# One two-input product for the softmax scaling, and two small statistics kept as extra columns, in a windowed attention that feeds a soft mixture of experts

## The chip, the core and the metric

The kernel runs on one core of one Trainium2 chip. The core has TensorE for matmuls (PE; its weight loads are listed as PEld), VectorE (DVE), ScalarE (ACT), GpSimd (POOL) and SyncE (SP), which here only issues transfers. The metric is the device time of one execution in microseconds (us). The kernel before took 297.65 us, the median of three runs of 295.35, 297.65 and 297.83 us.

## The reference

The program is an attention with a causal window of 128 positions and a linear distance bias per head, followed by a soft mixture of experts over all 4608 tokens (8 batches of 576).

```
scores = scale * q @ k.T ;  rel = i - j
scores = where((rel >= 0) & (rel < 128), scores - slope[h] * |rel|, -1e9)
attn   = exp(scores - max) ;  attn /= sum + 1e-9        # softmax along a row
x      = attn @ v                                        # 4608 tokens x 512
logits = x @ phi                                         # 32 slots
d = exp(logits - max over tokens) ;  d /= sum over tokens + 1e-9
slot_input = d.T @ x ;  slot_out = relu(slot_input @ w1) @ w2   # 8 experts, 4 slots each
c = exp(logits - max over slots)  ;  c /= sum over slots + 1e-9
out = c @ slot_out
```

## The kernel before, in words

A batch of 576 tokens is cut into four tiles of 128 tokens and a tail of 64. A tile's eight heads are done in two groups of four, the tail's in one, so that a batch has nine groups and the whole front part 72 (`groups`). One iteration of the loop over `groups` does these steps, each for another group, so that several groups are in flight:

- `softmax_front(new, old)` on DVE: `merge` (L267, L269, L271) masks the new scores in PSUM, `rowmax` (L289) takes each row's maximum, `inverse` (L301) turns the old group's row sums into reciprocals, `bias` (L292) scales the maximum for the exponential, and `normalise` (L306) multiplies the old group's four 128x128 blocks P, one instruction for each, by their reciprocals. `total` (L297) adds EPS to the sums, on GpSimd.
- `flip` (L351): four transposes of P on TensorE for the group three back. `split`: ScalarE copies the result to SBUF (L358), and GpSimd makes two masked copies of it with an affine select each (L360 for the part of the window in the previous tile, L362 for the part in its own; L365 and L367 for the tail).
- `values` (L387): P times v on TensorE for the group four back, which reads both masked copies; ScalarE stores the tile of x (`x_store`, L403).
- `scores` (L247 and L254, L235 and L240 in a batch's first tile) of the next group on TensorE.
- `expo` (L341): four exponentials on ScalarE, each with its row sums (the ACTIVATION_READ_ACCUMULATOR rows).

Beside that, once a batch, with steps spread over the iterations by `after_values`: x is flipped (`x_flip`, L408, kept by ScalarE at L417) and multiplied with phi (`logits`, L426; copied at L444 and L446). The statistics over tokens are kept as running values: `token_max` takes the maximum of the batch's logits (L451), joins it with the running one (L453) and negates it (L455). The running maximum stands in two columns that take turns, `mn` and `mo`. `token_exp` takes the exponentials on ScalarE (L475, L479), and `slot_add` (L522) adds the batch's share to the slots' inputs. The statistics over slots are in `ln`, 32 numbers for each token: `slots_max`, `slots_exp`, and `slots_norm`, which has four small DVE steps (L543 the sums, L544 adding EPS, L545 the reciprocals, L546 the product). These four go into a list `fillers`, of which `softmax_front` takes one at each of four places: behind `merge`, behind `rowmax`, behind `inverse` and behind `bias`.

The order on each engine is the order in which the code issues (`manual_schedule`): an engine works its list strictly from the front, and an instruction that waits holds up all behind it on that engine. The weights for the experts stream in all the while. After the front part come the experts (`hidden`, L931; `expert_out`, L967) and the mixing of their outputs (`combine`, L991, with copies at L993 and stores of the result).

Of the kernel before, what the change touches and what calls it, by code (L numbers as in the profile page):

```python
# [10 lines left out]
F32 = mybir.dt.float32  # L11
# [12 lines left out]
NS = E * SPE  # L24
P = 128
# [43 lines left out]
def tile_attn_softmoe(  # L69
# [24 lines left out]
    unit_r = cpool.tile([P, P], F32R, name="unit_r")  # L94
    ident = unit_r.bitcast(F32)
    fine = cpool.tile([P, 14], F32, name="fine")
    low, m_run, s_run = fine[:, 0:1], fine[:, 1:3], fine[:, 3:4]
    comb = cpool.tile([P, NS], F32, name="comb")
    phi = cpool.tile([P, NPAIR, NS], F32, name="phi")
    lg = cpool.tile([P, HW], F32, name="lg")  # L100
    ln = cpool.tile([P, NTT, NS], F32, name="ln")
    acc = cpool.tile([P, DM], F32, name="acc")
    kq = cpool.tile([P, 3 * UW], F32, name="kq")
    ramp = cpool.tile([P, 2, 2, WIN], BF16, name="ramp")
# [91 lines left out]
    with tc.manual_schedule(engines=ORDERED):  # L196
        warm = area[:, 2].bitcast(BF16)[:, 0:512]
        nc.vector.memset(warm, 0.0)
        nc.vector.memset(low, LOW)
        nc.vector.memset(ramp, 0.0)  # L200
        nc.vector.memset(ones, 1.0)
        nc.vector.memset(fine[:, 10:11], -1.0)
        nc.gpsimd.memset(cst[:, 0:P], 1.0)
        nc.gpsimd.affine_select(cst[:, 0:P], cst[:, 0:P], [[1, P]], ALU.is_gt, 0.0, base=0, channel_multiplier=-1)
        load_k(0, 0)
        load_q(0, nc.scalar)
        for par in range(2):
            nc.sync.dma_start(ramp[64 * par:64 * par + 1], slopes[par:par + 1])
        load_q(1, nc.scalar)
        load_q(2, nc.scalar)  # L210
        load_k(0, 1)
        tiny = work.tile([P, 1], F32, tag="nm", name="tiny")
        nc.scalar.activation(tiny, low, AF.Exp)
        for i in range(WARM):
            nc.tensor.matmul(free[i % 4], lhsT=warm[:, 0:P], rhs=warm, start=True, stop=True)
        nc.gpsimd.memset(lg, LOW)
        nc.gpsimd.memset(area[:, 3, 0:P], 1.0)
        nc.gpsimd.affine_select(
            unit_r, area[:, 3, 0:P], [[1, P]], ALU.is_equal, 0.0, base=0, channel_multiplier=-1)
        load_v()  # L220
        nc.scalar.dma_start(cst[:, P:], cstd)
        nc.scalar.dma_start(phi, phid)
        for t in range(2, NT):
            load_k(0, t)
# [75 lines left out]
    def inverse(key, us):  # L300
        nc.vector.reciprocal(st[key]["rs"][:, us], st[key]["rs"][:, us])  # L301

    def normalise(key, us, mul=nc.vector.tensor_scalar_mul):
        p4 = st[key]["p4"]
        for u in range(4)[us]:
            mul(p4[:, u], p4[:, u], st[key]["rs"][:, u:u + 1])  # L306

    fillers = []

# [4 lines left out]
    def softmax_front(new, old):  # L314
# [4 lines left out]
            total(old, ALL, nc.gpsimd)  # L319
        if first:  # L320
            inverse(old, ALL)
            normalise(old, LO, nc.scalar.mul)
        rowmax(new, ALL)
        filler()
        if not first and not eager:
# [93 lines left out]
    def lanes(b):  # L419
        return 4 if b < last else 2  # L420
# [11 lines left out]
    def with_tail(b):  # L432
        return b % 2 and b < last
# [12 lines left out]
            nc.scalar.copy(lg[fin, P:2 * P], lp[fin, P:2 * P])  # L446

    def token_max(b):
        odd, r = b % 2, NS * lanes(b)
        mo, mn = m_run[:, 1 - odd:2 - odd], m_run[:, odd:odd + 1]  # L450
        nc.vector.tensor_reduce(mn[0:r], lg[0:r, 0:P * (2 if with_tail(b) else 1)], axis=AX.X, op=ALU.max)  # L451
        if b:
            nc.vector.tensor_tensor(mn[0:r], mn[0:r], mo[0:r], op=ALU.max)  # L453
        nm = work.tile([P, 1], F32, tag="nm", name="nm")
        nc.vector.tensor_scalar_mul(nm[0:r], mn[0:r], -1.0)  # L455
        if r < P:
            nc.gpsimd.tensor_copy(mn[r:P], mo[r:P])
        st["n", b] = nm

    def slot_flip(b):  # L460
# [7 lines left out]
        st["c", b], st["lm"] = lq, dp  # L468

    def token_exp(b):  # L470
        odd, r = b % 2, NS * lanes(b)
        m = P * (2 if with_tail(b) else 1)
        nm = st.pop(("n", b))
        sb = work.tile([P, 1], F32, tag="sb", name="sb")
        nc.scalar.activation(lg[0:r, 0:m], lg[0:r, 0:m], AF.Exp, bias=nm[0:r], scale=1.0, accum_out=sb[0:r])  # L475
        al = None
        if b:
            al = work.tile([P, 1], F32, tag="al", name="al")
            nc.scalar.activation(al[0:r], m_run[0:r, 1 - odd:2 - odd], AF.Exp, bias=nm[0:r], scale=1.0)  # L479
        st["s", b] = (al, sb)  # L480

    def token_sum(b):
# [35 lines left out]
    def slot_add(b):  # L518
# [4 lines left out]
        else:  # L523
            nc.vector.tensor_copy(acc, ap)

    def slots(b):
        return ln[:, 9 * (b // 2) + 4 * (b % 2):9 * (b // 2) + 4 + 5 * (b % 2)]

    def slots_max(b):
        m = 4 + b % 2  # L530
# [8 lines left out]
    def slots_norm(b):  # L539
        m = 4 + b % 2  # L540
        cs = work.tile([P, 5], F32, tag="cs", name="cs")
        return [
            lambda: nc.vector.tensor_reduce(cs[:, 0:m], slots(b), axis=AX.X, op=ALU.add),  # L543
            lambda: nc.vector.tensor_scalar_add(cs[:, 0:m], cs[:, 0:m], EPS),  # L544
            lambda: nc.vector.reciprocal(cs[:, 0:m], cs[:, 0:m]),  # L545
            lambda: nc.vector.tensor_tensor(slots(b), slots(b), bc(cs[:, 0:m], 2, NS), op=ALU.mult),  # L546
        ]

    def later(fn, b):
# [12 lines left out]

    def lane_rows(to):
        lane_bank.extend([to[0:1, 0:2 * P], to[:, 2 * P:2 * P + 3]])
        nc.tensor.transpose(to[0:1, 0:P], m_run[:, last % 2:last % 2 + 1], ident)
        nc.tensor.transpose(to[0:1, P:2 * P], s_run, ident)

    def lane_values(i):
# [553 lines left out]
```

## Time and profile before

| | us |
|---|---|
| median of three runs | 297.65 |
| lowest and highest run | 295.35 and 297.83 |
| span of the profiled execution, first to last instruction | 294.4 |
| TensorE busy | 275.9 (94% of the span) |
| VectorE busy | 240.3 (82%) |
| ScalarE busy | 208.2 (71%) |
| GpSimd busy | 93.0 (32%) |

The profiled execution's own time outside its span is not shown; its span is 0.95 us under the fastest run and 3.25 us under the median. The loop over groups runs from about 6 to 222 us, the end of the front part to about 238.6 us, and the experts from there to the end. "Busy" is the time in which at least one instruction of an engine runs. Matmuls are pipelined and their ends are modelled, so TensorE's share can also hide short waits. A row of a timeline gives start, length, engine, line, operation, output and inputs, how many instructions are merged into it, and in brackets how long the engine was idle before and what ended that.

### The profile page before, as it was taken

The numbers are of one execution on the slowest core, as the hardware profiler recorded it, in microseconds if no ns is written. First come the engines' busy times: TensorE is split into PE (matmuls) and PEld (weight loads), VectorE is DVE, ScalarE is ACT, GpSimd is POOL, SyncE is SP. The second block draws the span as 40 slices with busy tenths as digits, with TensorE's granted clock in tenths as the row PEclk, the third lists the DMA queues.
The fourth block names the chain that finished last, engine by engine and source line by source line (L and its number), as shares of the span: only waits on it lengthen the run. The fifth ranks groups of instructions, "written<-read, shape, count | busy, mean of one in ns | idle before, by whom it ended". The sixth has DMA issues, their size and how long they took to land. (4 is left out here: it accounts for less than half of the span.)

```text
span 294.4 us, 13061 instructions
## 1 busy us (share of the span) xinstructions
PE 275.9 (94%) x5131; PEld 195.7 (66%) x5131; DVE 240.3 (82%) x745; ACT 208.2 (71%) x814; POOL 93.0 (32%) x207
## 2 busy tenths in 40 slices
PE   8598999999999999999999999999999999999980
PEld 4366777777677777776776777667766743587650
DVE  3889999999989999998999999979996454655450
ACT  2778898987988988987898978978886421044450
POOL 2033525542444354244415442445452011000000
PEclk9689999999999999999999999999999999999997
DMA  6635368878676887868588967776456599998997
GB/s 192 217 112 144 110 194 251 277 218 288 203 265 209 268 284 235 260 213 273 180 281 262 292 217 248 248 222 222 141 164 234 160 314 355 411 400 327 345 365 264
DMA packets 36754, 72.59 MB, mean 247 GB/s; under 512 B 4402, under 2 KB 15316, under 8 KB 36692
## 3 DMA queue, kind: packets, MB, share of 16 engines
q1 hardware_dynamic: 35972, 71.24, 72.8%
q8 instruction: 41, 0.67, 0.9%
q10 hardware_dynamic: 720, 0.51, 0.6%
q14 instruction: 21, 0.17, 0.2%
HBM read 62.29 MB, written 9.44 MB: 244 GB/s over the span
## 5 line engine op out<-in xcount | busy, mean ns | idle before, releaser
L341 ACT ACTIVATE area<-s,nb 128x128 f32<-128x128 f32 x288 | 102.3, 375 | 19.8 <-DVE nb L292 17.5
L306 DVE TENSOR_SCALAR area<-area,rs 128x128 f32<-128x128 f32 x286 | 79.5, 339 | 0.7 <-DVE nb L292 0.3
L387 PE MATMUL xp<-area 128*64 128x128 f32 (+1 forms) x1104 | 75.4, 272 | 1.1 <-POOL rs L297 0.4
L387 PEld LDWEIGHTS xp<-area 128*64 128x64 f32 x1104 | 56.5, 137 | 15.9 <-issue 9.3
L341 ACT ACTIVATION_READ_ACCUMULATOR area<-s,nb 128x1 f32 x288 | 61.3, 213 | 0.0
L289 DVE TENSOR_REDUCE s<-s 128x4 f32<-128x512 f32 x71 | 49.5, 698 | 2.2
L358 ACT COPY area<-pt 128x512 f32<-128x512 f32 (+1 forms) x72 | 42.3, 590 | 11.6 <-PE pt L351 11.3
L351 PE MATMUL pt<-unit_r,area 128*128 128x128 f32 x282 | 45.9, 285 | 2.7 <-ACT area L306 2.2
L297 POOL TENSOR_SCALAR rs<-sm 128x4 f32<-128x4 f32 x70 | 13.8, 197 | 99.0 <-ACT area L341 98.2
L351 PEld LDWEIGHTS pt<-unit_r,area 128*128 128x128 f32 x282 | 32.0, 143 | 17.2 <-PE s L254 5.0
L254 PE MATMUL s<-kq 64*32 64x160 f32 x1792 | 42.4, 303 | 0.1
L360 POOL TENSOR_SCALAR_AFFINE_SELECT area<-area 128x512 f32<-128x512 f32 x48 | 31.4, 655 | 26.7 <-ACT area L358 25.6
L269 DVE COPY_PREDICATED s<-cst,s 128x512 f32<-128x512 int32 x48 | 32.9, 686 | 1.3 <-PE s L254 1.3
L362 POOL TENSOR_SCALAR_AFFINE_SELECT area<-area 128x512 f32<-128x512 f32 x48 | 31.5, 657 | 3.3
L254 PEld LDWEIGHTS s<-kq 64*32 64x32 f32 x1792 | 29.9, 108 | 1.0 <-issue 0.4
L408 PE MATMUL xq<-unit_r,area 128*128 128x128 f32 x136 | 22.1, 285 | 0.8 <-ACT area L417 0.7
L403 ACT COPY area<-xp 128x512 f32<-128x512 f32 (+1 forms) x37 | 20.7, 559 | 2.9 <-PE xp L387 2.3
L247 PE MATMUL s<-ramp,ones 64*32 64x320 bf16 x448 | 18.9, 313 | 2.7 <-ACT area L341 2.2
L417 ACT COPY area<-xq 128x512 f32<-128x512 f32 x34 | 20.7, 608 | 0.2 <-PE xq L408 0.2
L408 PEld LDWEIGHTS xq<-unit_r,area 128*128 128x128 f32 x136 | 14.5, 141 | 7.4 <-issue 4.1
L993 ACT COPY ob<-po 128x512 f32<-128x512 f32 x19 | 10.4, 591 | 11.4 <-PE po L991 10.7
L993 DVE COPY ob<-po 128x512 f32<-128x512 f32 x17 | 11.2, 687 | 6.6 <-PE po L991 5.8
(169 smaller groups left out, 328.4 us busy)
## 6 DMA issues: line engine op xcount, KB each, us to landing
w<-w SPq DMA_DIRECT2D x53, 512.0 KB, 5.2
out<-ob SPq DMA_DIRECT2D x36, 256.0 KB, 3.9
kq<-q_t SPq DMA_DIRECT2D x69, 128.0 KB, 3.2
kq<-k_t SPq DMA_DIRECT2D x32, 256.0 KB, 3.8
area<-v_n SPq DMA_DIRECT2D x31, 256.0 KB, 4.2
area<-w SPq DMA_DIRECT2D x8, 512.0 KB, 4.8
area<-v_n SPq DMA_DIRECT2D x12, 128.0 KB, 3.1
kq<-w SPq DMA_DIRECT2D x3, 512.0 KB, 6.3
```

Source lines behind the costliest of these rows:

```text
L254: nc.tensor.matmul(s4[32 * c:32 * c + 32, 2 * par + jj, 32 * r:32 * r + WIN], lhsT=qt[rows, 2 * h + jj if t == 4 else jj, 32 * r:32 * r + 32],
L269: nc.vector.copy_predicated(s4[:, :, P:2 * P], bc(mask_u, 1, 4), s4[:, :, 0:P])
L289: nc.vector.tensor_reduce(st[key]["mx"][:, us], merged(key, us), axis=AX.X, op=ALU.max, negate=True)
L306: mul(p4[:, u], p4[:, u], st[key]["rs"][:, u:u + 1])
L341: nc.scalar.activation(s["p4"][:, u], merged(key, u), AF.Exp, bias=s["nb"][:, u:u + 1], scale=SCALE, accum_out=s["sm"][:, u:u + 1],)
L351: nc.tensor.transpose(s["pt"][:, u], s["p4"][:, u], ident)
L358: nc.scalar.copy(pa[:, us], s["pt"][:, us])
L360: nc.gpsimd.affine_select(pp[:, us], pa[:, us], [[0, m], [-1, P]], ALU.is_gt, 0.0, base=0, channel_multiplier=1)
L362: nc.gpsimd.affine_select(pa[:, us], pa[:, us], [[0, m], [1, P]], ALU.is_ge, 0.0, base=0, channel_multiplier=-1)
L387: nc.tensor.matmul(xp[D * par:D * par + D, j, 0:w], lhsT=v_slot[b, t - 1 + ph][0:rows, D * h:D * h + D], rhs=src[:, 2 * par + i] if t < 4 ...
L408: nc.tensor.transpose(xq[:, P * j:P * j + P], x_of(b, t)[:, j], ident)
L993: copy_by[by](ob, po)
```

## The change

Three things change. The product of P with its reciprocals becomes one `tensor_tensor` over all four blocks, whose second input is the column of reciprocals repeated along the row. Only the first two blocks of the very first group are still scaled one at a time on ScalarE. Then the running token maximum is stored in the column just ahead of the logits, in the same tile, so that one `tensor_reduce` over the logits and that column gives the joined maximum, already negated; GpSimd writes it back with its sign turned once `token_exp` has read the old one. And each token's 32 slot values get a 33rd column that holds EPS from the start, so that the sum includes it; the product of slot values and reciprocals goes to GpSimd for all batches but the last.

```diff
-    low, m_run, s_run = fine[:, 0:1], fine[:, 1:3], fine[:, 3:4]
+    low, s_run = fine[:, 0:1], fine[:, 3:4]
...
-    lg = cpool.tile([P, HW], F32, name="lg")
-    ln = cpool.tile([P, NTT, NS], F32, name="ln")
+    lgm = cpool.tile([P, 4 + HW], F32, name="lg")
+    m_run, lg = lgm[:, 3:4], lgm[:, 4:]
+    lne = cpool.tile([P, NTT, NS + 1], F32, name="ln")
+    ln = lne[:, :, 0:NS]
...
-        nc.gpsimd.memset(lg, LOW)
+        nc.gpsimd.memset(lgm, LOW)
+        nc.gpsimd.memset(lne[:, :, NS:NS + 1], EPS)
...
-    def normalise(key, us, mul=nc.vector.tensor_scalar_mul):
+    def normalise(key, us):
+        p4, rs = st[key]["p4"][:, us], st[key]["rs"][:, us]
+        nc.vector.tensor_tensor(p4, p4, bc(rs, 2, P), op=ALU.mult)
+
+    def normalise_first(key, us):
         p4 = st[key]["p4"]
         for u in range(4)[us]:
-            mul(p4[:, u], p4[:, u], st[key]["rs"][:, u:u + 1])
+            nc.scalar.mul(p4[:, u], p4[:, u], st[key]["rs"][:, u:u + 1])
...
     def token_max(b):
-        odd, r = b % 2, NS * lanes(b)
-        mo, mn = m_run[:, 1 - odd:2 - odd], m_run[:, odd:odd + 1]
-        nc.vector.tensor_reduce(mn[0:r], lg[0:r, 0:P * (2 if with_tail(b) else 1)], axis=AX.X, op=ALU.max)
-        if b:
-            nc.vector.tensor_tensor(mn[0:r], mn[0:r], mo[0:r], op=ALU.max)
+        r = NS * lanes(b)
         nm = work.tile([P, 1], F32, tag="nm", name="nm")
-        nc.vector.tensor_scalar_mul(nm[0:r], mn[0:r], -1.0)
-        if r < P:
-            nc.gpsimd.tensor_copy(mn[r:P], mo[r:P])
+        nc.vector.tensor_reduce(
+            nm[0:r], lgm[0:r, 3:4 + P * (2 if with_tail(b) else 1)], axis=AX.X, op=ALU.max, negate=True)
         st["n", b] = nm
...
-            nc.scalar.activation(al[0:r], m_run[0:r, 1 - odd:2 - odd], AF.Exp, bias=nm[0:r], scale=1.0)
+            nc.scalar.activation(al[0:r], m_run[0:r], AF.Exp, bias=nm[0:r], scale=1.0)
+        nc.gpsimd.tensor_scalar(m_run[0:r], nm[0:r], -1.0, 1.0, op0=ALU.mult, op1=ALU.mult)
...
     def slots_norm(b):
         m = 4 + b % 2
         cs = work.tile([P, 5], F32, tag="cs", name="cs")
+        mul = (nc.gpsimd if b < last else nc.vector).tensor_tensor
         return [
-            lambda: nc.vector.tensor_reduce(cs[:, 0:m], slots(b), axis=AX.X, op=ALU.add),
-            lambda: nc.vector.tensor_scalar_add(cs[:, 0:m], cs[:, 0:m], EPS),
+            lambda: nc.vector.tensor_reduce(cs[:, 0:m], lne[:, rows(b)], axis=AX.X, op=ALU.add),
             lambda: nc.vector.reciprocal(cs[:, 0:m], cs[:, 0:m]),
-            lambda: nc.vector.tensor_tensor(slots(b), slots(b), bc(cs[:, 0:m], 2, NS), op=ALU.mult),
+            lambda: mul(slots(b), slots(b), bc(cs[:, 0:m], 2, NS), op=ALU.mult),
         ]
```

The first place to look at is VectorE's list in the iteration of an even batch that takes the fillers. `area` holds P, `rs` its reciprocals, `s` the scores, `nb` the bias, `ln` and `cs` the slot values and their sums. Before:

```order
L267 COPY_PREDICATED s_1_83<-cst,fine 128x4x128
L543 TENSOR_REDUCE cs<-ln 128x4
L289 TENSOR_REDUCE s_1_83<-s_1_83 128x4
L544 TENSOR_SCALAR cs<-cs 128x4
L301 RECIPROCAL rs<-rs 128x4
L545 RECIPROCAL cs<-cs 128x4
L292 TENSOR_SCALAR nb<-s_1_83 128x4
L546 TENSOR_TENSOR ln<-ln,cs 128x128
L306 TENSOR_SCALAR area<-area,rs 128x128 x4
```

The same iteration on VectorE now:

```order
L270 COPY_PREDICATED s_1_83<-cst,fine 128x4x128
L550 TENSOR_REDUCE cs<-ln 128x4
L292 TENSOR_REDUCE s_1_83<-s_1_83 128x4
L551 RECIPROCAL cs<-cs 128x4
L304 RECIPROCAL rs<-rs 128x4
L295 TENSOR_SCALAR nb<-s_1_83 128x4
L308 TENSOR_TENSOR area<-area,rs 128x512
```

Between the masking and the bias the step that added EPS is gone, and the slots' reciprocals stand one place earlier; behind the bias the product of the slots is gone, and one product stands where four scalings stood.

The second place is GpSimd's list in the same iteration: `rs` are the sums of the group whose exponentials were taken last, and the pair of affine selects behind it makes the masked copies in `area` that `values` reads in the next iteration. Before:

```order
L297 TENSOR_SCALAR rs<-sm 128x4
L360 AFFINE_SELECT area<-area 128x512
L362 AFFINE_SELECT area<-area 128x512
L297 TENSOR_SCALAR rs<-sm 128x4
L365 AFFINE_SELECT area<-area 128x512
```

The same place on GpSimd now:

```order
L300 TENSOR_SCALAR rs<-sm 128x4
L552 TENSOR_TENSOR ln<-ln,cs 128x4x32
L367 AFFINE_SELECT area<-area 128x512
L369 AFFINE_SELECT area<-area 128x512
L300 TENSOR_SCALAR rs<-sm 128x4
L372 AFFINE_SELECT area<-area 128x512
```

The product of the slots now stands ahead of the pair of selects, and it waits for VectorE's reciprocals `cs`. In the same way the write of the running maximum (`lg<-nm 128x1`, L482 of the changed kernel) stands once a batch behind a pair of selects. TensorE's list is the same in both kernels.

More of the change, by code (lines that the diff above doesn't have):

```diff
@@ L321, in softmax_front @@
             inverse(old, ALL)
-            normalise(old, LO, nc.scalar.mul)
+            normalise_first(old, LO)
         rowmax(new, ALL)
@@ L470, in token_exp @@
     def token_exp(b):
-        odd, r = b % 2, NS * lanes(b)
+        r = NS * lanes(b)
         m = P * (2 if with_tail(b) else 1)
@@ L524, in slot_add, with rows @@
             nc.vector.tensor_copy(acc, ap)
+    def rows(b):
+        return slice(9 * (b // 2) + 4 * (b % 2), 9 * (b // 2) + 4 + 5 * (b % 2))
     def slots(b):
-        return ln[:, 9 * (b // 2) + 4 * (b % 2):9 * (b // 2) + 4 + 5 * (b % 2)]
+        return ln[:, rows(b)]
     def slots_max(b):
@@ L564, in lane_rows @@
         lane_bank.extend([to[0:1, 0:2 * P], to[:, 2 * P:2 * P + 3]])
-        nc.tensor.transpose(to[0:1, 0:P], m_run[:, last % 2:last % 2 + 1], ident)
+        nc.tensor.transpose(to[0:1, 0:P], m_run, ident)
         nc.tensor.transpose(to[0:1, P:2 * P], s_run, ident)
```

## Prediction

> **What bounds the kernel now.** I read the busy time by stage first: start, loop over groups, end of the front part, experts. The columns are TensorE, its weight loads, VectorE, ScalarE and GpSimd, each with busy us and instructions, then granted clock, DMA share and GB/s.
>
> ```profile
> core 0: us, PE busy (x) PEld busy (x) DVE busy (x) ACT busy (x) POOL busy (x), PEclk, DMA share, GB/s
> 0.00:30.00 30.00, 23.93 (x414) 16.20 (x415) 22.61 (x72) 19.75 (x81) 7.61 (x24) 0.89 0.57 169
> 30.00:210.00 180.00, 177.95 (x3668) 130.99 (x3666) 171.67 (x542) 155.02 (x638) 74.87 (x161) 1.00 0.74 236
> 210.00:238.60 28.60, 26.75 (x321) 19.11 (x320) 19.03 (x65) 18.52 (x67) 9.09 (x19) 1.00 0.60 195
> 238.60:294.40 55.80, 47.23 (x734) 29.41 (x733) 26.98 (x69) 14.89 (x30) 1.48 (x4) 0.96 0.93 349
> ```
>
> In the loop VectorE is busy 171.67 of 180 us, which by itself makes it look like the engine to relieve. But TensorE is busy 177.95, at full clock: only 2.05 us are left there. Since that share can hide waits, I looked next at TensorE's own timeline over one iteration.
>
> ```profile
> 110.44 0.60 PE L351 MATMUL pt<-unit_r,area 128*128 128x128 f32 x4
> ...
> 112.66 0.66 PE L351 MATMUL pt<-unit_r,area 128*128 128x128 f32 x4
> 113.24 1.09 PE L387 MATMUL xp<-area 128*64 128x128 f32 x16
> 114.33 0.33 PE L247 MATMUL s<-ramp,ones 64*32 64x320 bf16 x8
> 114.47 0.74 PE L254 MATMUL s<-kq 64*32 64x160 f32 x32
> 115.14 0.66 PE L408 MATMUL xq<-unit_r,area 128*128 128x128 f32 x4
> 115.63 0.60 PE L351 MATMUL pt<-unit_r,area 128*128 128x128 f32 x4
> 116.16 1.09 PE L387 MATMUL xp<-area 128*64 128x128 f32 x16
> ...
> 99.98 1.29 PE L254 MATMUL s<-kq 64*32 64x160 f32 x32
> ...
> 26.26 0.33 PE L247 MATMUL s<-ramp,ones 64*32 64x320 bf16 x8 [1.28 <-ACT area L341]
> ...
> 220.33 0.66 PE L408 MATMUL xq<-unit_r,area 128*128 128x128 f32 x4 [0.65 <-ACT area L417]
> ...
> 223.19 0.27 PE L465 MATMUL dp<-unit_r,lg 64*128 64x64 f32 x1 [0.62 <-ACT lg L444]
> ```
>
> From 112.66 to 116.16 each row begins before the one ahead has ended, or at once: TensorE works without a pause through a whole iteration. Hidden waits exist, but they are few: the 32 score matmuls take 0.74 us as a rule and 1.29 us at 99.98, so 0.55 us are hidden there. So two engines are nearly full, and the one that is not touched is the fuller. What the change can win is only TensorE's waits: 2.05 us in the loop and, as an estimate from rows like that at 99.98, as much again hidden; 28.60 − 26.75 = 1.85 us at the end of the front part; and the 1.28 us at 26.26. The sum, about 7 us, is the ceiling, however much VectorE gets back.
>
> **The change part by part.** First VectorE's durations. The groups' columns are count, busy us and mean ns; the timeline shows one scaling of P with GpSimd quiet, one with it at work, and the iteration with the fillers.
>
> ```profile
> L306 DVE TENSOR_SCALAR area<-area,rs 128x128 f32<-128x128 f32 x286 | 79.5, 339 | 0.7 <-DVE nb L292 0.3
> L691 DVE TENSOR_TENSOR cstk<-ln,cstk 128x256 fp32r<-128x256 f32 x9 | 3.8, 426 | 0.3
> L453 DVE TENSOR_TENSOR fine<-fine 128x1 f32<-128x1 f32 x6 | 2.1, 347 | 0.2
> L546 DVE TENSOR_TENSOR ln<-ln,cs 128x160 f32<-128x160 f32 x4 | 2.1, 527 | 0.0
> L546 DVE TENSOR_TENSOR ln<-ln,cs 128x128 f32<-128x128 f32 x4 | 2.0, 504 | 0.0
> L544 DVE TENSOR_SCALAR cs<-cs 128x5 f32<-128x5 f32 x4 | 1.5, 379 | 0.0
> L534 DVE TENSOR_TENSOR ln<-dp,cm 128x128 f32<-128x128 f32 x4 | 1.2, 292 | 0.1
> L544 DVE TENSOR_SCALAR cs<-cs 128x4 f32<-128x4 f32 x4 | 1.2, 301 | 0.0
> L455 DVE TENSOR_SCALAR nm<-fine 128x1 f32<-128x1 f32 x7 | 1.1, 154 | 0.2
> ```
>
> ```profile
> 112.61 1.25 DVE L306 TENSOR_SCALAR area<-area,rs 128x128 f32<-128x128 f32 x4
> 112.68 0.71 POOL L362 TENSOR_SCALAR_AFFINE_SELECT area<-area 128x512 f32<-128x512 f32 x1
> 113.78 0.69 DVE L267 COPY_PREDICATED s<-cst,fine 128x512 f32<-128x512 int32 x1
> 114.83 0.63 POOL L360 TENSOR_SCALAR_AFFINE_SELECT area<-area 128x512 f32<-128x512 f32 x1 [0.27 <-ACT area L358]
> 115.17 0.32 DVE L544 TENSOR_SCALAR cs<-cs 128x4 f32<-128x4 f32 x1
> 115.53 0.63 POOL L362 TENSOR_SCALAR_AFFINE_SELECT area<-area 128x512 f32<-128x512 f32 x1
> 115.73 0.57 DVE L546 TENSOR_TENSOR ln<-ln,cs 128x128 f32<-128x128 f32 x1
> 115.84 0.37 ACT L341 ACTIVATE area<-s,nb 128x128 f32<-128x128 f32 x1 [1.08 <-DVE nb L292]
> 116.23 0.86 DVE L306 TENSOR_SCALAR area<-area,rs 128x128 f32<-128x128 f32 x4
> ```
>
> The product of P. Four scalings take 0.86 us undisturbed (116.23) and 1.25 us beside a select of GpSimd (112.61); the mean is 79.5 / (286 / 4) = 1.11 us a group. No row shows the new product, 128x512. A product of 128 elements takes 292 ns and one of 256 takes 426 ns, so 134 ns for each 128 more, and 426 + 2 × 134 = 694 ns. It too has two SBUF inputs, and such a one waits for GpSimd: at 115.73 a product of 128 takes 0.57 us, 0.28 more than the 292 ns, and ends just behind the select that ends at 116.16. The bounds are 0.70 and 0.98 us; I take 0.90, nearer to the disturbed row because the iterations are alike. That is 0.21 us less in each of 70 groups, 14.7 us.
>
> The small steps. L453 and L455 vanish (2.1 + 1.1 us), as does L544 (1.5 + 1.2), and of L546 seven of eight products leave VectorE, all but one of 160 elements undisturbed (2.1 + 2.0 − 0.3). That is 9.7 us; the reductions grow by one column in 128 or by one in 32, which I cost at nothing. So VectorE goes from 240.3 to about 216 us, and in the loop from 171.7 to some 150 us, under ScalarE's 155.0. In time, this buys only what TensorE waited for on its account. Of the loop's 4 us I take half, 2.0: the waits come mostly through exponentials that start late, as at 115.84, where ScalarE stood 1.08 us for a bias that the fillers had delayed, and these start earlier now. Of the 1.28 us at 26.26 I take 0.5, since the exponentials there also queue behind a copy that waits for TensorE itself, and of the 0.65 and 0.62 us at the end of the front part 0.5, since the VectorE step ahead of them waits for matmuls. Gain: 3.0 us. Its bounds are 0 and 7.
>
> What GpSimd gets. Here are the nearest rows for its new work, and one select beside a VectorE instruction with two SBUF inputs.
>
> ```profile
> L204 POOL TENSOR_SCALAR_AFFINE_SELECT cst<-cst 128x128 f32<-128x128 f32 x1 | 0.3, 292 | 0.1
> L1023 POOL TENSOR_SCALAR ostk<-cst 128x64 fp32r<-128x64 f32 x2 | 0.7, 380 | 0.0
> L362 POOL TENSOR_SCALAR_AFFINE_SELECT area<-area 128x512 f32<-128x512 f32 x48 | 31.5, 657 | 3.3
> ```
>
> ```profile
> 215.90 0.69 DVE L267 COPY_PREDICATED s<-cst,fine 128x512 f32<-128x512 int32 x1
> 216.13 0.94 POOL L360 TENSOR_SCALAR_AFFINE_SELECT area<-area 128x512 f32<-128x512 f32 x1 [0.31 <-ACT area L358]
> ```
>
> The write of the running maximum, one column, stands behind a pair of selects and ahead of sums that wait for exponentials anyway: nothing, and 0.3 us a batch if that cover were gone. The product of the slots stands ahead of a pair of selects. It waits for VectorE's reciprocals, the selects queue behind it, and `values` on TensorE waits for them. Its own length lies between 0.29 us (one input, 128 elements) and 0.66 us; I take 0.45. In the iteration above, the reciprocals can come no earlier than 115.17 − 113.78 + 0.18 = 1.57 us behind the masking's start. That start is 113.78 because VectorE was late; scores were there by 112.7, so with the time won I put it at 113.1. Then the reciprocals are there at 114.7, the product ends at 115.2, the pair (0.63 + 0.07 + 0.63) at 116.5, and `values` wants its second half 0.1 us behind 116.16 (two of its 16 matmuls in 1.09 us): some 0.25 us late. If the product of P takes its turn between the two selects, they end 0.3 us later still (0.94 for 0.63 at 216.13). I take 0.5 us, bounds 0 and 0.9, in the three even batches of the loop; in odd ones a flip of x lies between and covers it. New waits: 1.5 us, bounds 0 and 5.
>
> The sum against the profiled execution: 294.4 − 3.0 + 1.5 = 292.9 us of span. What lies around the span isn't in the profile, and the fastest run is 0.95 us and the median 3.25 us above it, so I apply the difference of −1.5 us to the median: 297.65 − 1.5 = 296.1 us.
>
> **The rivals.** *All of it counts* (293.2 us). The selects start earlier by as much as they are delayed, and TensorE's visible waits of 2.05 + 1.85 us and 0.6 at the start go. For it speaks that ScalarE's copies ahead of the selects were themselves late behind late exponentials. Against it speaks that GpSimd's pair ends at 116.16, exactly where `values` begins: there is no slack today. 297.65 − 4.5 = 293.2.
>
> *GpSimd becomes the wait* (303 us, slower). Four short scalings let a select in between any two: at 112.68 it takes 0.71 us, hardly more than 0.63. One long product does not, and a select costs 0.3 us more, as at 216.13. If that reaches TensorE in half of the 48 pairs, it costs 7.2 us; with 1.5 for the slots and 3.0 won, 297.65 + 5.7 = 303. It decides where a pair ends more than 0.1 us behind the start of `values`. Against it: the pair has about an iteration of cover in most groups, and only the short iterations (one lasts from 110.44 to 112.66, 2.22 us) have none. The Trainium skill, page "SBUF — State Buffer", section "SBUF: two separate sides", says that VectorE with two SBUF inputs and GpSimd share a port pair as an exclusive lock, held for the whole instruction. By that rule the product of P shuts GpSimd out for all of its length, and the trace agrees at 216.13 in one direction and at 115.73 in the other.
>
> *The product isn't shorter* (299 us). If it loses its turn to both selects, it takes 0.70 + 2 × 0.28 = 1.26 us against 1.11; in some 62 groups of the loop that is 9 us more on VectorE against 8 saved by the small steps. VectorE stays full, the new waits stay, and nothing is won: 297.65 + 1.5. Against it: four scalings could lose four turns, one product hardly two. The Trainium skill, page "VectorE: DVE Perf Modes", section "The perf-mode tier table", gives fp32 scalings from SBUF twice the rate of a two-input product, which speaks against the change. With that page's formula of 58 cycles and one per element (half for the scaling), an estimate is 0.51 us for four scalings and 0.59 us for the product; the trace has 0.86 us for the four, so the fixed part of each weighs more here than the page says.
>
> **How the numbers follow.** Forecast 0.55 (its own range 294.3 to 298), all of it counts 0.27, GpSimd becomes the wait 0.12, the product isn't shorter 0.06. A difference under 1%, 3 us, can hardly be told from none here, as the three runs of before lie 2.5 us apart. Faster by over 1% (under 294.7) is the first rival and 0.05 of the forecast: 0.32. Slower by over 1% (over 300.6) is 0.10 of the second rival and 0.02 of the third: 0.12. The rest, 0.56, is within 1%. The range reaches from 292.6, a little under the first rival, to 300.0, which leaves out most of the second.
>
> **What would show it.** Right: the product of P at 0.7 to 1.0 us; VectorE at about 216 us busy and its share in the loop under ScalarE's; TensorE's steps as long as before and its busy time in the loop at 98% or more, so that the span moves little; in even batches a wait of `values` for the second select behind the slots' product. Wrong: `values` waiting for selects in many iterations; the product over 1.1 us; a slots' product on GpSimd of over 1 us; or TensorE's steps themselves getting shorter, which would mean that what I read as its own rate was a wait in disguise, and that the ceiling of 7 us was none.

## The result and the profile after

The changed kernel takes 298.34 us, the median of 20 runs (296.65 to 301.40). The kernel before takes 296.83 us in 20 runs on the same chip (294.61 to 302.44). The ratio is 1.0061, with a 95% interval of 1.0040 to 1.0082. So the kernel became slower by 0.6%, about 1.8 us. That is within the 1% called "the same" above, but the forecast was 1.5 us faster.

The profiled execution has a span of 296.3 us, against 294.4 before. The busy time by stage, with the columns and stages of the first table in the prediction, now reads:

```profile
0.00:30.00 30.00, 22.91 (x426) 15.47 (x427) 21.51 (x53) 21.05 (x87) 9.95 (x26) 0.94 0.56 172
30.00:210.00 180.00, 174.99 (x3580) 127.30 (x3578) 153.78 (x337) 153.64 (x628) 85.90 (x170) 1.00 0.74 235
210.00:240.60 30.60, 29.31 (x401) 20.90 (x396) 18.18 (x46) 19.26 (x72) 10.44 (x23) 1.00 0.56 178
240.60:296.30 55.70, 47.58 (x737) 29.72 (x736) 26.67 (x67) 14.91 (x30) 1.96 (x5) 0.96 0.93 355
```

In the loop VectorE went from 171.67 to 153.78 us of 180, so the relief that was meant is there. TensorE went from 177.95 to 174.99, which is 97% of the stretch: it waits 3 us more, and gets through 3580 of its instructions in this stretch, where it was 3668. GpSimd went from 74.87 to 85.90. The groups of VectorE and GpSimd that moved, each with count, busy us and mean ns, then idle time before and what ended it:

```profile
L308 DVE TENSOR_TENSOR area<-area,rs 128x512 f32<-128x512 f32 x70 | 59.1, 845 | 2.0
L270 DVE COPY_PREDICATED s<-cst,fine 128x512 f32<-128x512 int32 x15 | 12.5, 835 | 0.0
L489 DVE SCALAR_TENSOR_TENSOR fine<-fine,al,sb 128x1 f32<-128x1 f32 x6 | 3.5, 583 | 0.0
```

```profile
L369 POOL TENSOR_SCALAR_AFFINE_SELECT area<-area 128x512 f32<-128x512 f32 x48 | 36.2, 754 | 3.3
L367 POOL TENSOR_SCALAR_AFFINE_SELECT area<-area 128x512 f32<-128x512 f32 x48 | 35.4, 738 | 29.2 <-ACT area L365 26.2 <-PE xp L394 2.8
L374 POOL TENSOR_SCALAR_AFFINE_SELECT area<-area 64x512 f32<-64x512 f32 x7 | 6.9, 991 | 0.5
L552 POOL TENSOR_TENSOR ln<-ln,cs 128x128 f32<-128x128 f32 x4 | 1.6, 400 | 6.1 <-DVE cs L551 4.2 <-DVE rs L304 1.8
L552 POOL TENSOR_TENSOR ln<-ln,cs 128x160 f32<-128x160 f32 x3 | 1.4, 456 | 1.9 <-DVE rs L304 1.9
L482 POOL TENSOR_SCALAR lg<-nm 128x1 f32<-128x1 f32 x7 | 1.3, 184 | 0.0
```

The product of P takes 0.845 us, where four scalings took 1.11. Against that, the selects of GpSimd grew from about 655 ns to 738 and 754, and the tail's from 663 to 991. The slots' product takes 0.40 us for a batch of four tiles and 0.46 us for one of five, and GpSimd stood idle ahead of it for VectorE's reciprocals.

To see where the time went, I matched TensorE's 5131 weight loads of the two traces, which come in the same order, and took for each the difference of its start. Negative is earlier than before. The table has the larger steps, not all:

| place (us in the trace after) | shift ahead, us | shift behind, us | step |
|---|---|---|---|
| first 34 us | 0 | −1.33 | −1.33 |
| iteration with the fillers, batch at 60 | −0.86 | −0.05 | +0.81 |
| the same, at 90 | −0.61 | +0.24 | +0.85 |
| the same, at 116 | −0.33 | +0.44 | +0.77 |
| the same, at 145 | −0.11 | +0.74 | +0.85 |
| `values` at 158 | +0.46 | +1.60 | +1.14 |
| fillers, at 173 | +1.33 | +2.11 | +0.78 |
| fillers, at 202 | +1.56 | +2.27 | +0.71 |
| `values` at 209 | +2.27 | +2.71 | +0.44 |
| end of the front part | +2.71 | +2.21 | −0.50 |

The six iterations that take the fillers lose 0.7 to 0.9 us each, 4.8 us together, odd batches as much as even ones. Between them 0.3 to 0.6 us are won back, and 0.47 us of the lead at 34 us is lost again by 60. Of what is won back between 90 and 116, 0.49 us is not the change's: it is the row at 99.98 in the prediction, 32 score matmuls in 1.29 us. They take 0.73 us here and in all nine experiments below, whether P has one product, two, four scalings or none, so that wait belongs to the one execution of the kernel before that was profiled.

```profile
99.92 0.73 PE L257 MATMUL s<-kq 64*32 64x160 f32 x32
```

This is the first of the six iterations; a timeline's columns are those of the prediction:

```profile
58.46 0.20 POOL L300 TENSOR_SCALAR rs<-sm 128x4 f32<-128x4 f32 x1 [0.73 <-ACT area L348]
58.99 0.16 DVE L551 RECIPROCAL cs<-cs 128x4 f32<-128x4 f32 x1
59.24 0.40 POOL L552 TENSOR_TENSOR ln<-ln,cs 128x128 f32<-128x128 f32 x1 [0.59 <-DVE rs L304]
59.32 0.86 DVE L308 TENSOR_TENSOR area<-area,rs 128x512 f32<-128x512 f32 x1
59.59 1.09 POOL L367 TENSOR_SCALAR_AFFINE_SELECT area<-area 128x512 f32<-128x512 f32 x1
...
60.74 0.44 PE L394 MATMUL xp<-area 128*64 128x128 f32 x4 [0.25 <-POOL area L367]
60.75 0.64 POOL L369 TENSOR_SCALAR_AFFINE_SELECT area<-area 128x512 f32<-128x512 f32 x1
...
61.45 0.88 PE L394 MATMUL xp<-area 128*64 128x128 f32 x12 [0.27 <-POOL area L369]
```

GpSimd has done the sums by 58.66 and then waits 0.59 us for VectorE, with the two selects queued behind. The slots' product runs from 59.24. When it ends, VectorE's product of P, which started at 59.32, is still running, and the first select takes 1.09 us instead of 0.64: it ends 0.50 us behind the end of the product of P at 60.18. `values` (L394) waits for the first select and then again for the second; the two waits are 0.52 us of the step, and its 16 matmuls, cut in two, take 0.44 + 0.88 = 1.32 us instead of 1.09. An odd batch looks the same:

```profile
88.25 0.46 POOL L552 TENSOR_TENSOR ln<-ln,cs 128x160 f32<-128x160 f32 x1 [0.63 <-DVE rs L304]
88.66 1.09 POOL L367 TENSOR_SCALAR_AFFINE_SELECT area<-area 128x512 f32<-128x512 f32 x1
...
90.51 0.88 PE L394 MATMUL xp<-area 128*64 128x128 f32 x12 [0.27 <-POOL area L369]
```

The two steps in `values` itself, at 158 and 209, are of another kind:

```profile
158.34 0.44 PE L394 MATMUL xp<-area 128*64 128x128 f32 x4 [0.87 <-issue]
...
209.47 0.88 PE L394 MATMUL xp<-area 128*64 128x128 f32 x12 [0.96 <-DMA area<-v_n]
```

At 209 the wait is for a block of v. Five of the experiments below wait there too, 0.92 to 1.50 us, the longest in the kernel that changes only the token column; three others wait 0.16 to 0.39 us. The kernel without scaling and the kernel before show no such wait in their one trace each. At 158 the row names no releaser, and what it waits for stays open. A row without a releaser at that place is 0.55 us long in one experiment and 0.27 in another, and none stands there in the others. Neither wait follows the change, and I did not test them.

### The profile page after: what moved, and what is told of

Its sections match the earlier page's. It is cut to its first block, busy times and chain, and to the rows that moved or that the text cites. A ratio compares the mean times of both kernels' runs of the same rounds, so it can differ in the third digit from the quotient of the medians.

```text
span 296.3 us, 12828 instructions
## 1 busy us (share of the span) xinstructions
PE 274.8 (93%) x5131; PEld 193.4 (65%) x5131; DVE 220.1 (74%) x502; ACT 208.9 (70%) x814; POOL 108.3 (37%) x222
## 5 line engine op out<-in xcount | busy, mean ns | idle before, releaser
L394 PE MATMUL xp<-area 128*64 128x128 f32 (+1 forms) x1104 | 77.1, 273 | 5.0 <-POOL area L369 1.6
L394 PEld LDWEIGHTS xp<-area 128*64 128x64 f32 x1104 | 56.1, 136 | 21.9 <-issue 10.2
L348 ACT ACTIVATION_READ_ACCUMULATOR area<-s,nb 128x1 f32 x288 | 63.3, 220 | 0.0
L308 DVE TENSOR_TENSOR area<-area,rs 128x512 f32<-128x512 f32 (+1 forms) x73 | 60.4, 828 | 2.1
L358 PE MATMUL pt<-unit_r,area 128*128 128x128 f32 x282 | 45.2, 282 | 3.6 <-ACT area L313 2.6
L367 POOL TENSOR_SCALAR_AFFINE_SELECT area<-area 128x512 f32<-128x512 f32 x48 | 35.4, 738 | 29.2 <-ACT area L365 26.2
L257 PE MATMUL s<-kq 64*32 64x160 f32 x1792 | 41.1, 298 | 0.0
L369 POOL TENSOR_SCALAR_AFFINE_SELECT area<-area 128x512 f32<-128x512 f32 x48 | 36.2, 754 | 3.3
L257 PEld LDWEIGHTS s<-kq 64*32 64x32 f32 x1792 | 29.2, 106 | 0.6 <-issue 0.2
L270 DVE COPY_PREDICATED s<-cst,fine 128x512 f32<-128x512 int32 (+1 forms) x17 | 13.4, 788 | 3.9 <-issue 3.9
```

The lines of the kernel that those rows point to most:

```text
L257: nc.tensor.matmul(s4[32 * c:32 * c + 32, 2 * par + jj, 32 * r:32 * r + WIN], lhsT=qt[rows, 2 * h + jj if t == 4 else jj, 32 * r:32 * r + 32],
L308: nc.vector.tensor_tensor(p4, p4, bc(rs, 2, P), op=ALU.mult)
L348: nc.scalar.activation(s["p4"][:, u], merged(key, u), AF.Exp, bias=s["nb"][:, u:u + 1], scale=SCALE, accum_out=s["sm"][:, u:u + 1],)
L358: nc.tensor.transpose(s["pt"][:, u], s["p4"][:, u], ident)
L367: nc.gpsimd.affine_select(pp[:, us], pa[:, us], [[0, m], [-1, P]], ALU.is_gt, 0.0, base=0, channel_multiplier=1)
L369: nc.gpsimd.affine_select(pa[:, us], pa[:, us], [[0, m], [1, P]], ALU.is_ge, 0.0, base=0, channel_multiplier=-1)
```

## The experiments

My theory was that the slots' product, by its place in GpSimd's list, is the loss: it waits for VectorE ahead of the urgent selects. The rival was the product of P: long and with two SBUF inputs, it holds up GpSimd's selects everywhere. Ratios are to the kernel before in runs on the same chip, with 95% intervals. The first four kernels ran on one chip (before: 296.06 us, 30 runs), the next four on another (before: 295.93 us, 35 runs), the last on a third.

### The slots' product stays on VectorE

```diff
-        mul = (nc.gpsimd if b < last else nc.vector).tensor_tensor
+        mul = nc.vector.tensor_tensor
```

> The changed kernel with the slots' product on VectorE for all batches (in its place among the fillers); the rest as changed. Queue theory: in the changed kernel the product of the slots stands ahead of the pair of selects on GpSimd and waits for VectorE's reciprocals, and this costs TensorE 0.8 us in each of six iterations. Without it the waits of values behind late selects in these iterations vanish, 6 x 0.8 = 4.8 us less, and VectorE gets back 0.3 to 0.6 us an iteration that it can spare: 293.5 to 294.5 us, 1% under the kernel before. Port theory: what costs is the long product of P, which holds the port against the selects everywhere; then nothing much changes, 298 us.

Measured: 295.35 us, ratio 0.9970 (0.9945 to 0.9994). All of the change except this one move is 0.3% faster than before; so the loss comes with the move. The time is nearer to the queue theory, but under neither expectation: the waits behind the slots' product are gone, while each of the six tails of the loop now loses some 0.3 us, as in the next kernel.

### The product of P alone

The kernel before, with the new `normalise` and nothing else of the change.

```diff
-    def normalise(key, us, mul=nc.vector.tensor_scalar_mul):
+    def normalise(key, us):
+        p4, rs = st[key]["p4"][:, us], st[key]["rs"][:, us]
+        nc.vector.tensor_tensor(p4, p4, bc(rs, 2, P), op=ALU.mult)
...
-            mul(p4[:, u], p4[:, u], st[key]["rs"][:, u:u + 1])
+            nc.scalar.mul(p4[:, u], p4[:, u], st[key]["rs"][:, u:u + 1])
```

> The kernel before with the one product for P alone; token maximum and slots as before. Queue theory: only gains are left, the faster start and the shorter waits for late exponentials: 1.5 to 2.5 us under the kernel before, 294.5 to 295.5. Port theory: the loss is all here, 1 to 2 us over the kernel before.

Measured: 296.50 us, ratio 1.0002 (0.9977 to 1.0027). That is between the two expectations, and neither came true. VectorE is busy 225.3 us instead of 240.3, and none of it arrives. The groups and one tail of a batch show a part of what takes it. First the kernel with the product alone, groups and then the timeline:

```profile
L305 DVE TENSOR_TENSOR area<-area,rs 128x512 f32<-128x512 f32 x70 | 55.3, 791 | 2.2 <-DVE nb L292 1.0
L366 POOL TENSOR_SCALAR_AFFINE_SELECT area<-area 128x512 f32<-128x512 f32 x48 | 35.7, 743 | 3.3
L371 POOL TENSOR_SCALAR_AFFINE_SELECT area<-area 64x512 f32<-64x512 f32 x7 | 7.2, 1026 | 0.5
```

```profile
62.92 0.69 DVE L305 TENSOR_TENSOR area<-area,rs 128x512 f32<-128x512 f32 x1
63.12 1.02 POOL L371 TENSOR_SCALAR_AFFINE_SELECT area<-area 64x512 f32<-64x512 f32 x1
...
64.19 1.47 PE L391 MATMUL xp<-area 64*64 64x64 f32 x28 [0.42 <-POOL area L371]
```

And the same place in the kernel before:

```profile
63.79 1.34 DVE L306 TENSOR_SCALAR area<-area,rs 128x128 f32<-128x128 f32 x4
63.80 0.66 POOL L367 TENSOR_SCALAR_AFFINE_SELECT area<-area 64x512 f32<-64x512 f32 x1
```

Who yields has changed. Beside four short scalings the select went at full speed (0.66 us) and VectorE paid (1.34 instead of 0.86). Here the one product, which started first, goes at full speed (0.69) and the select pays (1.02). In most iterations the select has time to spare; in the tail it has none, and `values`, which ran on there without such a wait, waits 0.42 us. By the shifts of TensorE's weight loads, this kernel loses 0.36 to 0.39 us in each of the six tails of the loop. It is also 0.9 us ahead of before at 34 us; that this lead comes from the product is not shown (see below, on the gain). In the changed kernel the tail's select is as slow, but it starts at 62.48 instead of 63.12, since the exponentials come earlier, and `values` hardly waits. The groups of the tail's matmuls, first with the product alone, then in the changed kernel:

```profile
L391 PE MATMUL xp<-area 64*64 64x64 f32 x112 | 6.3, 230 | 2.7 <-POOL area L371 2.7
L394 PE MATMUL xp<-area 64*64 64x64 f32 x112 | 6.3, 230 | 0.2 <-POOL area L374 0.2
```

### The slots' product on GpSimd alone

The kernel before, with this one move.

```diff
-            lambda: nc.vector.tensor_tensor(slots(b), slots(b), bc(cs[:, 0:m], 2, NS), op=ALU.mult),
+            lambda: (nc.gpsimd if b < last else nc.vector).tensor_tensor(slots(b), slots(b), bc(cs[:, 0:m], 2, NS), op=ALU.mult),
```

> The kernel before with the slots' product on GpSimd alone (EPS still added by its own VectorE step, four scalings of P). Queue theory: the loss is here, 3 to 5 us over the kernel before, 300 to 302, since the reciprocals come even later than in the changed kernel. Port theory: within 0.5 us of the kernel before.

Measured: 299.57 us, ratio 1.0107 (1.0070 to 1.0145), 3.2 us slower. Here P still has its four scalings, so the rival's mechanism is not in this kernel at all, and the loss is.

```profile
60.45 0.43 POOL L546 TENSOR_TENSOR ln<-ln,cs 128x128 f32<-128x128 f32 x1 [1.11 <-DVE nb L292]
60.84 0.63 POOL L360 TENSOR_SCALAR_AFFINE_SELECT area<-area 128x512 f32<-128x512 f32 x1
61.53 0.44 PE L387 MATMUL xp<-area 128*64 128x128 f32 x4 [0.57 <-POOL area L360]
...
62.30 0.88 PE L387 MATMUL xp<-area 128*64 128x128 f32 x12 [0.33 <-POOL area L362]
```

GpSimd waits 1.11 us here, since VectorE still has the step that adds EPS, and `values` waits 0.57 us and 0.33 us, though the selects keep nearly their length (654 and 663 ns in the mean). So the wait for VectorE is enough for a loss of this size, without a select that is drawn out.

### The slots' product behind the selects

The changed kernel, in which the product of slots and reciprocals stays on GpSimd but is issued behind the pair of selects of the same iteration (for the first six batches).

```diff
-            lambda: mul(slots(b), slots(b), bc(cs[:, 0:m], 2, NS), op=ALU.mult),
...
+    def slots_scale(b):
+        m = 4 + b % 2
+        nc.gpsimd.tensor_tensor(slots(b), slots(b), bc(st["cs", b][:, 0:m], 2, NS), op=ALU.mult)
...
+            if b < last - 1:
+                do("act", i + 7, slots_scale, b)
```

> The changed kernel with the slots' product still on GpSimd, but issued behind the pair of selects of the same iteration (for the loop's six batches). Queue theory: its inputs are there by then and nothing urgent is queued behind it, so the 4.8 us go: 293 to 294.5 us. Port theory: the same instructions hold the port for the same time, 298 us.

Measured: 294.55 us, ratio 0.9934 (0.9905 to 0.9963). The same work on the same engine, one place further back: 1.27% less than the changed kernel, 3.8 us, with the two intervals put together 2.7 to 4.8 us.

```profile
59.41 0.63 POOL L367 TENSOR_SCALAR_AFFINE_SELECT area<-area 128x512 f32<-128x512 f32 x1 [0.27 <-ACT area L365]
59.83 0.76 DVE L308 TENSOR_TENSOR area<-area,rs 128x512 f32<-128x512 f32 x1
60.12 0.97 POOL L369 TENSOR_SCALAR_AFFINE_SELECT area<-area 128x512 f32<-128x512 f32 x1
60.39 0.60 PE L358 MATMUL pt<-unit_r,area 128*128 128x128 f32 x4
...
60.92 1.09 PE L394 MATMUL xp<-area 128*64 128x128 f32 x16
61.06 0.39 POOL L560 TENSOR_TENSOR ln<-ln,cs 128x128 f32<-128x128 f32 x1
```

The first select starts at 59.41, at once when ScalarE's copy is there, and runs ahead of the product of P. The second pays 0.34 us for the port and still ends in time: the 16 matmuls of `values` run in their 1.09 us without a pause.

### Ahead of the selects, but with its inputs ready

Is it the wait for VectorE or the product's own 0.40 us? Three empty fillers put the slots' product one iteration later, still between the sums and the selects.

```diff
+        skip = [lambda: None] * (3 if b < last - 1 else 0)
...
+            *skip,
```

> The changed kernel with the slots' product still on GpSimd and still between the sums and a pair of selects, but one iteration later, so that VectorE's reciprocals are there long before GpSimd comes to it. If the cost is the wait for the reciprocals (about 0.6 us of the 0.8 us an iteration), it falls to what its own 0.4 us push the selects back: 294.5 to 296 us, 1% under the changed kernel. If the cost is its length and the port behind it, it stays: 297.5 to 298.5 us.

Measured: 294.99 us, ratio 0.9956 (0.9935 to 0.9976), which is 1.05% or 3.1 us (2.2 to 4.0) less than the changed kernel.

```profile
61.61 0.19 POOL L300 TENSOR_SCALAR rs<-sm 128x4 f32<-128x4 f32 x1 [0.38 <-ACT area L348]
61.88 0.40 POOL L554 TENSOR_TENSOR ln<-ln,cs 128x128 f32<-128x128 f32 x1
```

The product no longer waits, and most of the loss is gone. The iteration is another one too, that of the tail, so this is not the wait alone; but the product's own length in front of selects costs little.

### The slots' product behind the selects, and four scalings of P

The kernel with the slots' product behind the selects, with the old four scalings put back.

```diff
-        p4, rs = st[key]["p4"][:, us], st[key]["rs"][:, us]
-        nc.vector.tensor_tensor(p4, p4, bc(rs, 2, P), op=ALU.mult)
+        p4 = st[key]["p4"]
+        for u in range(4)[us]:
+            nc.vector.tensor_scalar_mul(p4[:, u], p4[:, u], st[key]["rs"][:, u:u + 1])
```

> The kernel with the slots' product behind the selects (e5), but P scaled again by four instructions. If the one product for P is what wins there, this goes back to the kernel before, 296 us. If it wins by the small steps that left VectorE, and the product of P gains and loses alike, this stays near 294.5 us.

Measured: 294.31 us, ratio 0.9931 (0.9902 to 0.9960): the same as with one product (0.9934), on another chip; the two intervals together leave about 1.2 us either way. VectorE is busy 235.2 us here and 219.6 there, and nothing of that difference of 15.6 us can be seen in the time.

```profile
L309 DVE TENSOR_SCALAR area<-area,rs 128x128 f32<-128x128 f32 x286 | 83.7, 354 | 1.0
L370 POOL TENSOR_SCALAR_AFFINE_SELECT area<-area 128x512 f32<-128x512 f32 x48 | 31.8, 662 | 3.3
```

With four scalings the second select is back at 662 ns; with one product it took 785 in the kernel with the slots' product behind the selects.

### The product of P in two halves

Behind the selects again, with two products of 128x256 for a group.

```diff
-        p4, rs = st[key]["p4"][:, us], st[key]["rs"][:, us]
-        nc.vector.tensor_tensor(p4, p4, bc(rs, 2, P), op=ALU.mult)
+        for part in ((LO, HI) if us == ALL else (us,)):
+            p4, rs = st[key]["p4"][:, part], st[key]["rs"][:, part]
+            nc.vector.tensor_tensor(p4, p4, bc(rs, 2, P), op=ALU.mult)
```

> The kernel with the slots' product behind the selects (e5), and the product of P in two halves of 128x256, each 0.42 us. If the long hold of the port still costs something in e5, GpSimd gets a select in between and it is 0.5 to 1.5 us faster than e5, 293 to 294. If not, it is e5's time, or up to 0.5 us over it.

Measured: 294.65 us, ratio 0.9964 (0.9944 to 0.9984). It lets the selects in (691 ns instead of 785), VectorE pays (228.5 us busy), and the time is no better than with one product or with four scalings; the three intervals overlap.

### The token maximum as a column, alone

The kernel before, with only the running maximum moved beside the logits and the joined, negated reduce.

```diff
+        nc.vector.tensor_reduce(
+            nm[0:r], lgm[0:r, 3:4 + P * (2 if with_tail(b) else 1)], axis=AX.X, op=ALU.max, negate=True)
...
+        nc.gpsimd.tensor_scalar(m_run[0:r], nm[0:r], -1.0, 1.0, op0=ALU.mult, op1=ALU.mult)
```

> The kernel before with the token maximum as a column beside the logits, and nothing else. Two VectorE steps less and one GpSimd step more in each of eight batches, off the path on both theories: within 0.5 us of the kernel before.

Measured: 295.92 us, ratio 0.9993 (0.9968 to 1.0018). Neither the two instructions saved nor the write on GpSimd can be seen in the time.

### No scaling of P at all

To measure the ceiling, the kernel before leaves out the multiplication of P by its inverse sums, except where the first and the last group do it apart.

```diff
-            normalise(old, HI if first else ALL)
+            if first:
+                normalise(old, HI)
```

> The kernel before without the scaling of P for all groups but the first and the last (its output is not the reference's): some 77 of VectorE's 240 us are left out, and no two-port instruction of P meets a select. If TensorE's own rate is the bound, as the prediction read it, this is the most that any change to the scaling can win, and it is at most 7 us: 289 to 293 us. If TensorE's steps were waits for VectorE in disguise, it falls by 10 us or more, under 286.

Measured: 290.71 us, of four runs, against 296.34 on that chip, ratio 0.983 (0.978 to 0.988), so some 5 us (3.6 to 6.5). VectorE falls from 240.3 to 172.0 us. In the loop (columns as above):

```profile
30.00:210.00 180.00, 178.82 (x3729) 132.72 (x3730) 115.73 (x311) 156.61 (x649) 74.41 (x163) 1.00 0.74 240
```

TensorE is busy 178.82 of 180 us with VectorE at 115.73: there is little left to gain in the loop from VectorE once it has been relieved of 68 us.

## Why the prediction was wrong

**The bound and the ceiling: right.** TensorE sets the time, and I put what VectorE's relief could win at 7 us at most. Taking the whole scaling away wins some 5 us, with TensorE busy 99% of the loop; in the changed kernel it is 97%, where I had named 98% or more. The scaling and the small steps together were not left out in one kernel. One of the ceiling's terms was misread: the 0.55 us hidden at 99.98 is in no other trace, so what I put down as "as much again hidden" rests on a single wait. The warning sign that I named, TensorE's steps themselves getting shorter, did not come: `flip` takes 0.60 us and `values` 1.09 us where nothing disturbs them (at 60.39 and 60.92 in the kernel with the slots' product behind the selects), as before.

**The product of P, its length: right, its use: wrong.** Forecast 0.70 us undisturbed and 0.90 in the mean; measured 0.69 (at 62.92, above) and 0.845. VectorE was forecast at 216 us and in the loop at 150, under ScalarE; it has 220.1 and 153.78, level with ScalarE's 153.64. The product saved more than I took (1.11 − 0.845 = 0.27 us for each of the 70, not 0.21), but two groups took 15 × 0.146 + 6 × 0.376 = 4.4 us back: the masking (L270, 835 ns against 689) and the one-column update (L489, 583 against 207). The few us that are still between I did not follow. But the product alone gives 1.0002, and putting the four scalings back into the best kernel changes nothing that can be seen. I had the exchange in the prediction, a select that pays 0.3 us where P's product pays nothing, only as a rival's price, not in the forecast's gain. In the traces the one that starts later pays: the select from 59.59 ends 0.50 us behind the product that ends at 60.18, and in the tail of the changed kernel a product that starts during a select takes 0.96 us instead of 0.69.

```profile
61.74 0.67 POOL L372 TENSOR_SCALAR_AFFINE_SELECT area<-area 128x512 f32<-128x512 f32 x1
61.99 0.96 DVE L308 TENSOR_TENSOR area<-area,rs 128x512 f32<-128x512 f32 x1
```

The Trainium skill, page "SBUF — State Buffer", section "SBUF: two separate sides", calls the shared port pair an exclusive lock that whoever starts first holds for the whole instruction, and these rows agree. One long instruction in place of four short ones did not remove the waiting of the two engines for each other here; it changed which of them waits. The one that was relieved was VectorE, which has time, and the one that waits feeds `values`.

**The gain of 3.0 us: too high, and for another reason.** The kernel with the slots' product in a harmless place is 0.66% faster, 2.0 us (1.1 to 2.8). Of my three parts, the end of the front part gave 0.5 us as forecast (−0.50 in the table): the waits of 0.65 and 0.62 us are 0.54 and 0.24. At the start I took 0.5 us of the wait of 1.28 us at 26.26, and that wait is still there, in the changed kernel as in all nine experiments:

```profile
25.33 0.33 PE L250 MATMUL s<-ramp,ones 64*32 64x320 bf16 x8 [1.29 <-ACT area L348]
```

What gave the lead of 1.33 us at 34 us is not shown. The kernel with the token column alone, which keeps the four scalings, has a lead of 1.27 us there, and the one with P's product in two halves is 0.45 us behind. The granted clock of the first 30 us is 0.94 in the changed kernel against 0.89 before, and also 0.94 with the token column alone, so the lead need not come from the change at all. The token column is worth nothing that can be measured. In the loop, the three kernels with the slots' product behind the selects win 0.2 us right behind five of the six iterations with the fillers, with one product of P, with two and with four scalings, some 1.1 us in all; with the token column alone this is missing. So what is left, by elimination and by these steps, are the slots' steps that VectorE no longer has. That such parts add up is assumed.

**The new waits: the step that failed.** "I take 0.5 us ... in the three even batches of the loop; in odd ones a flip of x lies between and covers it", together 1.5 us with bounds of 0 and 5. The trace has 0.7 to 0.9 us in all six batches, 4.8 us, and moving the product one place back returns 3.8 us. So the mechanism was in the prediction, and the term was mis-sized: six iterations at 0.8 us in place of three at 0.5. Two things made it so. First, the odd batches: the reciprocals are late there too (GpSimd waits 0.63 us at 88.25), and the flip of x covers nothing of it. It could not set odd batches apart: a flip of x stands in the even iteration that the prediction shows, at 115.14. Second, the two costs add up in one iteration: the slots' product waits until VectorE has finished its small steps, and by then VectorE starts the product of P, so the first select runs into it. I had that as a possible 0.3 us in the second select; it was 0.45 in the first. How the loss divides between the wait and the drawn-out select was not measured apart: with four scalings and the longer wait of 1.11 us, the wait alone loses as much. The gain of 2.0 us and the 3.8 us of the place are measured on the same kernel with the product behind the selects, so that they add up to the +1.8 us of the result is no test of its own.

**The rivals.** "GpSimd becomes the wait" named the right engine and the right sign, but its mechanism, P's product in half of the 48 pairs at 7.2 us, is refuted by the product alone at 1.0002; what remains of it are the tails of that kernel, some 0.4 us each, and in the changed kernel hardly those. "All of it counts" put the gain at 4.5 us; even the version behind the selects, without the new waits, has 2.0. "The product isn't shorter" is refuted by 0.845 us. Undisturbed, the product takes 0.69 us and four scalings take 0.86, and the difference bought no time. The estimate in the prediction had them the other way round, 0.59 and 0.51. It used a row of the Trainium skill, page "VectorE: DVE Perf Modes", section "The TRN2 errata — SBUF-src ops pay a fixed extra latency per instruction", and overlooked that the page itself, right below that row, calls it too low and gives 691 ns for an fp32 `tensor_tensor` of 512 elements. That is what the trace shows (0.69 us at 62.92), so the fixed part does not weigh more here than the page says.

**What stays open.** The waits of `values` at 158 and 209 in the trace of after, 1.6 us together, were not tested. Without them the span would lie near that of before, but the ratio of the medians, over 20 runs, includes whatever they do on average. What else sets the product alone back to the time of before, and what the lead at the start comes from, is open too.

The best versions are the two with the slots' product behind the selects, with one product of P or with four scalings. Both are about 0.7% faster than the kernel before and 1.3% faster than the changed one.

## What to carry to other kernels

An instruction moved to an idle engine brings its waits with it, and on an engine that works its list in order they are paid by whatever stands behind: give it a place behind the urgent work, or where its inputs are long there (moving one 0.4 us product behind the selects, six times in the program, returned 3.8 us). Where instructions of two engines hold each other up, one long instruction in place of several short ones changes who waits; look at the slack of the other engine before counting the saving. A wait that stands in a single trace, like the one at 99.98, is no wait to count on. And where the bounding engine is another one, measure the ceiling by leaving the work out: 68 us less on VectorE were worth 5 us.

## What the runs showed of the hardware

Instructions of VectorE that were not changed became longer: the one-column update (L489) rose from 207 to 583 ns and the masking with a constant from SBUF (L270) from 689 to 835 ns. The masking takes 836 ns with P's product alone and 690 with the slots' product alone, but 860 ns in the kernel that does not scale P at all. So it does not need the product: it is long where it starts during a select of GpSimd. The one-column update is back at 207 and 208 ns where P is scaled in two halves or by four instructions. Two such pairs, from the changed kernel and from the one without scaling:

```profile
56.76 0.97 POOL L369 TENSOR_SCALAR_AFFINE_SELECT area<-area 128x512 f32<-128x512 f32 x1
57.16 1.13 DVE L270 COPY_PREDICATED s<-cst,fine 128x512 f32<-128x512 int32 x1
...
55.12 0.63 POOL L363 TENSOR_SCALAR_AFFINE_SELECT area<-area 128x512 f32<-128x512 f32 x1
55.27 1.03 DVE L267 COPY_PREDICATED s<-cst,fine 128x512 f32<-128x512 int32 x1 [0.87 <-PE s L240]
```

GpSimd's two-input product takes 400 ns for 128 elements in a row and 456 ns for 160, so 56 ns for 32 elements; an estimate from these two lengths alone is a fixed part of some 180 ns. A one-input instruction of one column takes 184 ns there. Four short scalings of VectorE beside a select let it pass nearly undisturbed (0.66 us) and are drawn out themselves (1.34 us), while one instruction of the same work, where it starts first, goes undisturbed (0.69 us) and draws out the select to 1.02 us.
